# A new order of operations in the first block of a linear-attention and feed-forward kernel

## The chip, the cores and the metric

The kernel runs on one core of a Trainium2 chip. The metric is the device time of one launch in microseconds (us).

## The reference

The inputs are r, k, v of shape (4 batches, 8 heads, 768 positions, 48), a decay w and a bonus u for each head and channel, and two weight matrices, w_in (384 x 2048) and w_out (2048 x 384), all in float32. The kernel has to compute

```python
for t in range(768):                       # for each batch and head
    cur = outer(u * k[t], v[t])
    y[t] = r[t] @ (state + cur)
    state = w[:, None] * state + outer(k[t], v[t])
x = y as (3072 tokens, 384)
h = x @ w_in
g = where(h > 0, h, exp(min(h, 0)) - 1)
out = g @ w_out
```

## The kernel before

The 768 positions are cut into six token blocks of 128 positions. A block n holds 128 positions of all four batches, so 512 tokens. A *unit* (n, b) is the attention of one batch in one block. A block's feed-forward layer goes in 16 *steps* f, one for each 128 rows of the hidden layer. While the layer of one block runs, the attention of the next block is made between its matmuls. All matrices are split into a high and a low part, so every product is three matmuls.

The order of all work is written out by hand, as strings of short names that a loop reads in each step. Each engine runs its own instructions in the order in which the names stand, so a name that stands behind another on the same engine waits until that one is done. `START` makes the four units of block 0. `FIRST` is the order of each of the 16 steps of block 0's layer: it makes the units of block 1, one after the other, four steps each. Unit b has its stages 0 to 3 in the steps 4b to 4b+3, and the last character of a name is the stage in which it acts. `LATER` is the order of the steps of the blocks 1 to 5, in which the units of the blocks 2 to 5 are made at times taken from tables (`A` the step of the scores, `T` of the transposes, `Y` of the outputs, with an offset).

The names that matter, by engine:

- TensorE (PE): `hid` the hidden product of step f (9 matmuls of 512 columns), `T` the transposes of r and k of a unit, `A` its scores, `Y` its outputs, `proj` the output projection of one step before (two before from step 6 on).
- ScalarE (ACT): `neg` is a Relu and then the exponential of the hidden product, `sp` the cast that gives the high part of one weight tile (and two GpSimd instructions for the other), `gh` the high part of the activated tile, `wd` the widening of the next weights, whose data a DMA brings, `Eq` the diagonal of the odd heads' scores, `xh` the high part of x.
- VectorE (DVE): `ma` merges the halves of the weights that `wd` has widened, `r4d` the low part of a weight tile, `elu` the activation, `gl` the low part of the activated tile, `rud` the products r * u * k of a unit (two multiplies), `sum` their sum, `dr` and `dk` the decayed r and k that the scores need, `krd` the decayed k for the state, `swd` the decayed state, `pa` and `pb` the masking of a unit's scores (its outputs need both), `xl` the low part of x, `ns` the new state, `tT` transposes of a later unit.
- GpSimd (POOL): `Dp` the diagonal of the even heads' scores, `r3` the low part of the other weight tile.
- SyncE's queue (SP), which issues the DMAs one after the other: `Lw` loads the weights for five steps on (five DMAs), `rk` and `v` load r, k and v of a later unit, `mb` moves blocks of a transposed unit to DRAM (4 DMAs), `mr` gathers them again, `G` moves part of a finished x to other partitions (6 DMAs, `fill_x`), `Gl` is the same function for the last unit of a block.

The weight staging holds three pairs of tiles. `Lw` of step f needs the pair that step f has just used, and its data are widened by `wd` of step f+2. The hidden product of a block needs x of all four units of the block, with the moves of `G`. A gathered unit (`mr`) is decayed by VectorE and GpSimd one step ahead of its scores.

Of the kernel before, what the change touches and what calls it, by code (L numbers as in the profile page):

```python
# [20 lines left out]
B, H, S, D = 4, 8, 768, 48  # L21
# [29 lines left out]


FIRST = """
Eq1 rud0 hid ns3 A1 T0 ma sp sum0 neg r4d elu dk0 Y2 xh2 pb1 mbT+1 rk3 xl2 G2 mrT+1 proj gh
Dp0 pa1 dr0 r3 gl krd0 swd1 v3 rudA-2 wd Lw third tT+0
"""
LATER = """
hid AY tT+0 pbA+2 bkA-1 brA-1 proj neg elu gh gl st nsY+0 xhY+0 xlY+0 paA+1 EqA+1 krA+1 mbT+0 mrT+0 rudA-2
swA+2 sumA-1 rkY+0 vY+0 GlY+0 GY+1 DpA+0 out
"""  # L60
SCORES = [17, 20, 23, 26] + [13 + 4 * j for j in range(4, 16)]
OUTPUTS = SCORES[1:] + [77]
# [4 lines left out]
class Kernel:  # L67
# [314 lines left out]
            self.load_weights(j)  # L382

    def stages(self, n, f):
        return [(f - 4 * b, 1, b) for b in range(B) if n == 0 and 0 <= f - 4 * b < 4]

    def units_at(self, times, step):
        return [divmod(2 * B + j, B) for j, t in enumerate(times) if t == step]
# [13 lines left out]
    def step(self, n, f):  # L402
        nc = self.nc

        k = f + 2 if n == 0 else NF + 1
        units = self.stages(n, f)


        last = divmod(n * NF + f - (1 if (n, f) < EARLY else 2), NF)
        both = {  # L410
            "ru": lambda n, b: self.current(n, b),
            "kr": lambda n, b: self.key_rest(n, b),
            "A": lambda n, b: self.scores(n, b),
            "sw": lambda n, b: self.decay_state(n, b),
            "rk": lambda n, b: self.load_after(n, b, self.load_rk),
            "ns": lambda n, b: self.new_state(n, b),
            "v": lambda n, b: self.load_after(n, b, self.load_v),
            "sum": lambda n, b: self.current_sum(n, b),
            "Dp": lambda n, b: self.diag_scores(n, b, 0),
            "Dq": lambda n, b: self.diag_scores(n, b, 1),  # L420
            "Ep": lambda n, b: self.diag_scores(n, b, 0, True),
            "Eq": lambda n, b: self.diag_scores(n, b, 1, True),
            "rud": lambda n, b: self.current(n, b, nc.vector),
            "krd": lambda n, b: self.key_rest(n, b, nc.vector),
            "swd": lambda n, b: self.decay_state(n, b, nc.vector),
            "pa": lambda n, b: self.take_scores(n, b, 0),
            "pb": lambda n, b: self.take_scores(n, b, 1),
            "Y": lambda n, b: self.outputs(n, b),
            "xh": lambda n, b: self.split_x(n, b, 0),
            "xl": lambda n, b: self.split_x(n, b, 1),  # L430
            "G": lambda n, b: self.fill_x(n, b) if n == 1 or b < B - 1 else None,
            "Gl": lambda n, b: self.fill_x(n, b) if b == B - 1 else None,
        }
        by_pe = {
            "T": lambda n, b: self.turn_in(n, b),
            "dr": lambda n, b: self.decay_r(n, b),
            "dk": lambda n, b: self.decay_k(n, b),
        }
        moved = {
            "t": lambda n, b: self.turn_blocks(n, b),  # L440
            "mb": lambda n, b: self.move_blocks(n, b),
            "mr": lambda n, b: self.gather_blocks(n, b),
            "br": lambda n, b: self.decay_moved(n, b, 0),
            "bk": lambda n, b: self.decay_moved(n, b, 1),
        }
        layer = {
            "hid": lambda: self.hidden(n, f, self.rest_of(n, f)),
            "ma": lambda: self.merge(k),
            "neg": lambda: self.negative(n, f),
            "sp": lambda: self.split_w(k),  # L450
            "r4": lambda: self.rest_w(k, 1),
            "r3": lambda: self.rest_w(k, 0),
            "r4d": lambda: self.rest_w(k, 1, nc.vector),
            "r3d": lambda: self.rest_w(k, 0, nc.vector),
            "elu": lambda: self.elu(n, f),
            "gh": lambda: self.split_g(n, f, 0),
            "gl": lambda: self.split_g(n, f, 1),
            "proj": lambda: self.project(*last) if last in self.g else None,
            "Lw": lambda: [self.load_weights(j) for j in (2 * k + 2 * DEEP - 1, 2 * k + 2 * DEEP) if n == 0],
            "wd": lambda: self.widen(k + 1),  # L460
            "st": lambda: self.store(last[0]) if last[1] == NF - 1 and last[0] in self.acc else None,
            "out": lambda: self.store_next(),
            "third": lambda: self.third_slot() if (n, f) == (0, 14) else None,
            "AY": lambda: self.insertion(now),
        }
        now = n * NF + f
        for op in (LATER if n else FIRST).split():
            if op in layer:
                layer[op]()
                continue  # L470
            if op[-2] in "+-":
                name, times = op[:-3], {"A": SCORES, "Y": OUTPUTS, "T": TURNS}[op[-3]]
                for m, b in self.units_at(times, now - int(op[-2:])):
                    if (name, m, b) not in self.done:
                        self.done.add((name, m, b))
                        {**both, **moved}[name](m, b)
                continue
            name, stage = op[:-1], int(op[-1], 16)
            for at, m, b in units:
                todo = {**both, **by_pe}  # L480
                if at == stage and name in todo and (name, m, b) not in self.done:
                    self.done.add((name, m, b))
                    todo[name](m, b)
# [681 lines left out]
```

## Time and profile before

| | us |
|---|---|
| median of 3 runs | 520.05 |
| lowest and highest run | 519.72 and 521.48 |
| the profiled execution | 518.8 |
| its span, first to last instruction | 517.1 |
| TensorE busy | 499.7 |
| VectorE busy | 307.3 |
| ScalarE busy | 244.8 |
| GpSimd busy | 125.2 |

The time is that of the whole launch; the span lies inside it, from the first to the last instruction of the core. Busy times are sums over the instructions of an engine; TensorE's matmuls overlap each other, and the ends of matmuls are modelled. The mean granted clock of TensorE was 0.992 of full speed.

### The profile page before, as it was taken

Reading aid. Unit: us, or ns where it says so; the run is one execution under the profiler, and the core shown is the slowest. Engines: PE = TensorE matmul, PEld = TensorE weight load, DVE = VectorE, ACT = ScalarE, POOL = GpSimd, SP = SyncE. Lnnn points to the kernel's source line nnn. Section 1 sums busy time; section 2 is a strip of 40 time slices with the busy share of each in tenths; the row PEclk is TensorE's granted clock in tenths of the full one; section 3 lists DMA queues with packets and bytes.
Section 4 is the critical chain, followed back from the end, with each engine's and each line's share of the span. In section 5 each row is a group of like instructions: output and inputs, shape, how many; then the busy total and the mean of one; then the engine's idle time right before and its main releaser. Section 6 shows DMA issues by size and latency. Waiting matters only on the chain.

```text
span 517.1 us, 9430 instructions
## 1 busy us (share of the span) xinstructions
PE 499.7 (97%) x3584; PEld 412.7 (80%) x3584; DVE 307.3 (59%) x529; ACT 244.8 (47%) x463; POOL 125.2 (24%) x151
## 2 busy tenths in 40 slices
PE   8998997999999998999999999999999999999995
PEld 6987775878778886878888788888888887799995
DVE  5787777686667765665655765655765533433332
ACT  3267566564444454354355354454444454354442
POOL 5845546453223312112112112111011000000000
PEclk9999998999999999999999999999999999999999
DMA  9986679575854546157346156356154000011001
GB/s 134 201 169 172 121 182 179 124 137 126 153 124 99 129 103 136 45 121 150 72 83 133 46 117 137 75 97 133 46 118 113 16 10 10 1 30 25 9 0 67
DMA packets 114204, 50.92 MB, mean 98 GB/s; under 512 B 91362, under 2 KB 110052, under 8 KB 114148
## 3 DMA queue, kind: packets, MB, share of 16 engines
q1 hardware_dynamic: 102052, 45.49, 43.0%
q10 hardware_dynamic: 12096, 4.72, 3.9%
q8 instruction: 30, 0.49, 0.4%
q14 instruction: 26, 0.21, 0.1%
HBM read 35.12 MB, written 13.11 MB: 93 GB/s over the span
## 4 chain that ended last, share of the span: by engine, by line
PE 80%; DVE 7%; ACT 4%; DMA 4%; issue 2%; POOL 1%; SPq 1%; ACTq 0%; DVEq 0%; POOLq 0%
PE ps_acc L1082 35%; PE ps_h L1040 33%; PE ps_y L800 4%; PE ps_a L767 3%; DMA stage<-in_moe_w_in_dram 2%; DVE ps_h L1055 1%; PE ps_y L855 1%; PE ps_y L775 1%; DVE g L1063 1%; ACT g L1050 1%; PE ps_y L924 1%; DVE stage L563 1%; ACT g L1049 1%; ACT g L1061 1%; DMA rk<-blocks 1%
## 5 line engine op out<-in xcount | busy, mean ns | idle before, releaser
L1040 PE MATMUL ps_h<-x,wh 128*128 128x512 f32 (+1 forms) x588 | 180.9, 389 | 2.1 <-DMA x<-x 1.8
L1082 PE MATMUL ps_acc<-g,wh 128*128 128x512 f32 x480 | 167.3, 403 | 0.0
L1055 DVE SCALAR_TENSOR_TENSOR ps_h<-g,ps_h 128x512 f32<-128x512 f32 x96 | 66.6, 693 | 120.9 <-ACT g L1050 120.9
L1040 PEld LDWEIGHTS ps_h<-x,wh 128*128 128x128 f32 x588 | 109.1, 188 | 27.0 <-DVE g L1063 3.2
L1040 PE MATMUL ps_h<-x,wl 128*128 128x512 f32 (+1 forms) x294 | 113.6, 386 | 0.6 <-DVE wl L601 0.6
L1049 ACT ACTIVATE g<-ps_h 128x512 f32<-128x512 f32 x96 | 57.2, 596 | 115.4 <-PE ps_h L1040 103.3
L1082 PEld LDWEIGHTS ps_acc<-g,wh 128*128 128x128 f32 x480 | 90.8, 189 | 21.8 <-issue 1.1
L1063 DVE TENSOR_TENSOR g<-ps_h,g 128x512 fp32r<-128x512 f32 x96 | 66.3, 690 | 54.8 <-ACT g L1061 54.1
L1061 ACT CAST g<-ps_h 128x512 fp32r<-128x512 f32 x96 | 56.3, 586 | 82.9 <-DVE ps_h L1055 82.9
L1082 PE MATMUL ps_acc<-g,wl 128*128 128x512 f32 x240 | 94.6, 394 | 0.0
L1040 PEld LDWEIGHTS ps_h<-x,wl 128*128 128x128 f32 x294 | 55.2, 188 | 12.7 <-DVE wl L601 0.8
L1050 ACT ACTIVATE g<-g 128x512 f32<-128x512 f32 x96 | 60.7, 632 | 3.1
L819 POOL TENSOR_TENSOR a<-ident,diag 128x512 f32<-128x512 f32 x20 | 20.9, 1044 | 150.2 <-PE ps_y L800 131.8
L1082 PEld LDWEIGHTS ps_acc<-g,wl 128*128 128x128 f32 x240 | 45.6, 190 | 9.1
L660 POOL TENSOR_TENSOR tb<-rk,qw 128x512 f32<-128x512 f32 x16 | 21.8, 1361 | 78.8 <-DMA rk<-blocks 55.3
L1082 PE MATMUL ps_acc<-wh,g 128*128 128x384 f32 x128 | 35.0, 337 | 0.1
L574 POOL TENSOR_SCALAR stage<-stage 128x384 f32<-128x384 f32 x16 | 19.7, 1231 | 42.4 <-DVE stage L563 42.4
L826 DVE COPY_PREDICATED a<-mask,ps_a 128x512 f32<-128x512 int32 x40 | 27.4, 728 | 0.0
L815 ACT ACTIVATE a<-ident,diag 128x128 f32<-128x128 f32 x80 | 25.5, 393 | 0.0
L767 PEld LDWEIGHTS ps_a<-stage,tb 48*64 48x64 f32 x512 | 20.3, 133 | 5.6 <-issue 5.3
L767 PE MATMUL ps_a<-stage,tb 48*64 48x128 f32 x512 | 24.7, 273 | 0.0
L1082 PEld LDWEIGHTS ps_acc<-wh,g 128*128 128x128 f32 x128 | 23.4, 188 | 1.2 <-issue 0.5
(128 smaller groups left out, 488.0 us busy)
## 6 DMA issues: line engine op xcount, KB each, us to landing
blocks<-tb SPq DMA_DIRECT2D x64, 128.0 KB, 2.3
rk<-blocks SPq DMA_DIRECT2D x16, 512.0 KB, 3.6
stage<-in_moe_w_out_dram SPq DMA_DIRECT2D x16, 383.8 KB, 4.9
stage<-in_moe_w_in_dram SPq DMA_DIRECT2D x32, 143.7 KB, 4.6
out_dram<-stage ACTq DMA_DIRECT2D x80, 48.0 KB, 1.7
r_t<-in_r_dram SPq DMA_DIRECT2D x17, 192.0 KB, 4.5
k_t<-in_k_dram SPq DMA_DIRECT2D x17, 192.0 KB, 5.2
v_t<-in_v_dram SPq DMA_DIRECT2D x17, 192.0 KB, 5.3
```

The source lines that it names most:

```text
L660: (self.nc.gpsimd if i else self.nc.vector).tensor_mul(dst, src, by)
L767: nc.tensor.matmul(un["pa"][i][keys, a * P : (a + 1) * P], lhsT=un["k"][rows, a, keys], rhs=un["r"][rows, a, :], start=True, stop=True, sk ...
L815: self.nc.scalar.activation(un["a"][i][:, a, :], self.ident, AF.Copy, scale=diag[:, a : a + 1])
L819: self.nc.gpsimd.tensor_mul(un["a"][i], self.ident.unsqueeze(1).to_broadcast([P, HP, P]), diag.unsqueeze(2).to_broadcast([P, HP, P]),)
L826: self.nc.vector.copy_predicated(un["a"][i], self.mask.bitcast(I32).unsqueeze(1).to_broadcast([P, HP, P]), un["pa"][i].rearrange("p (a t) ...
L1040: self.nc.tensor.matmul(ph[:, part], lhsT=a[:, c * P : (c + 1) * P], rhs=x[:, c, part], start=(c == 0 and i == 0), stop=(c == NC - 1 and i ...
L1049: nc.scalar.activation(g, ph, AF.Relu, scale=-1.0)
L1050: nc.scalar.activation(g, g, AF.Exp, scale=-1.0)
L1055: self.nc.vector.scalar_tensor_tensor(ph, g, -1.0, ph, op0=ALU.add, op1=ALU.max)
L1061: nc.scalar.copy(part, g)
L1063: nc.vector.tensor_sub(part, g, self.g[n, f][2].bitcast(F32))
L1082: self.nc.tensor.matmul(at, lhsT=lhs, rhs=rhs, start=(f == 0 and i == 0), stop=(f == NF - 1 and i == 2),)
```

## The change

In `FIRST`, four things change their place.

- `sp` (the weights' cast) and `r4d` stood ahead of `elu`, and `sp` ahead of `neg`; now the order is `neg`, `elu`, `sp`, `r4d`. On ScalarE the Relu and the exponential come ahead of the cast, on VectorE the activation ahead of the weights' low part.
- VectorE's work for a unit is spread: `rud` of the units 1 to 3 goes to the end of the step ahead of stage 0 (`rudx`), `krd` from stage 0 to stage 1, `swd` from stage 1 to stage 2. The first unit keeps `rud` in stage 0.
- `gh` stands ahead of `xh` on ScalarE. On VectorE `gl` stands ahead of `xl`, of both masks `pa` and `pb`, and of both decays `dk` and `dr`; before, it stood behind them. The first unit has both decays (`df`) ahead of `elu`.
- `proj` stands after `mr` in the text; on TensorE its place among the matmuls is the same.

In `LATER`, `Gl` is moved from behind the loads `rk` and `v` to a place ahead of `mr`, and it now serves all units from (2, 3) on. Before, only the last unit of a block was served by `Gl`, and the others by `G` one step later.

```diff
 FIRST = """
-Eq1 rud0 hid ns3 A1 T0 ma sp sum0 neg r4d elu dk0 Y2 xh2 pb1 mbT+1 rk3 xl2 G2 mrT+1 proj gh
-Dp0 pa1 dr0 r3 gl krd0 swd1 v3 rudA-2 wd Lw third tT+0
+Eq1 hid ns3 A1 T0 rud0 ma sum0 neg df0 elu sp r4d Y2 gh gl xh2 xl2 pa1 pb1 dk0 dr0 mbT+1 rk3 G2 mrT+1
+proj krd1 swd2 Dp0 r3 rudx v3 rudA-2 wd Lw third tT+0
 """
 LATER = """
-hid AY tT+0 pbA+2 bkA-1 brA-1 proj neg elu gh gl st nsY+0 xhY+0 xlY+0 paA+1 EqA+1 krA+1 mbT+0 mrT+0 rudA-2
-swA+2 sumA-1 rkY+0 vY+0 GlY+0 GY+1 DpA+0 out
+hid AY tT+0 pbA+2 bkA-1 brA-1 proj neg elu gh gl st nsY+0 xhY+0 xlY+0 paA+1 EqA+1 krA+1 mbT+0 GlY+0 mrT+0 rudA-2
+swA+2 sumA-1 rkY+0 vY+0 GY+1 DpA+0 out
 """
...
-        return [(f - 4 * b, 1, b) for b in range(B) if n == 0 and 0 <= f - 4 * b < 4]
+        return [(f - 4 * b, 1, b) for b in range(B) if n == 0 and -1 <= f - 4 * b < 4]
...
-            "G": lambda n, b: self.fill_x(n, b) if n == 1 or b < B - 1 else None,
-            "Gl": lambda n, b: self.fill_x(n, b) if b == B - 1 else None,
+            "G": lambda n, b: self.fill_x(n, b) if (n, b) < (2, B - 1) else None,
+            "Gl": lambda n, b: self.fill_x(n, b) if (n, b) >= (2, B - 1) else None,
...
-            "dr": lambda n, b: self.decay_r(n, b),
-            "dk": lambda n, b: self.decay_k(n, b),
+            "dk": lambda n, b: self.decay_k(n, b) if b else None,
+            "dr": lambda n, b: self.decay_r(n, b) if b else None,
+            "df": lambda n, b: self.decay_in(n, b) if b == 0 else None,
...
-            name, stage = op[:-1], int(op[-1], 16)
+            name, stage = op[:-1], -1 if op[-1] == "x" else int(op[-1])
```

## Rows read from the trace of the kernel before

**Rows 1.** TensorE's waits, whole span: waiting line, releaser, us in total, times, longest.

```profile
PE ps_a L741 <- DVE rk L672: 5.9, 3, 3.3
PE ps_h L1040 <- DMA x<-x: 1.8, 2, 1.6
```

**Rows 2.** Windows, the stretch of step 9: length, busy by engine, PEclk, DMA share, GB/s.

```profile
80.67:92.36 11.69, 8.35 (x35) 6.57 (x35) 9.70 (x17) 7.47 (x15) 6.54 (x7) 0.72 1.15 228
```

**Rows 3.** TensorE's timeline: start, us, line, operation, count, idle before and releaser.

```profile
86.34 2.08 PE L741 MATMUL ps_a<-rk 48*128 48x128 f32 x16 [3.33 <-DVE rk L672]
88.35 0.79 PE L1082 MATMUL ps_acc<-g,wh 128*128 128x512 f32 x1
...
123.93 0.68 PE L1040 MATMUL ps_h<-x,wh 128*128 128x512 f32 x2
...
206.33 0.70 PE L1040 MATMUL ps_h<-x,wh 128*128 128x512 f32 x2 [1.58 <-DMA x<-x]
```

**Rows 4.** VectorE's timeline, steps 6, 8, 13 and 29.

```profile
67.57 1.35 DVE L826 COPY_PREDICATED a<-mask,ps_a 128x512 f32<-128x512 int32 x2
...
80.53 0.55 DVE L703 TENSOR_TENSOR ru<-r_t,u_b 128x384 f32<-128x384 f32 x1
...
81.59 0.95 DVE L563 SCALAR_TENSOR_TENSOR stage<-stage,wide 128x768 int32<-128x768 int32 x1
...
84.31 0.69 DVE L1055 SCALAR_TENSOR_TENSOR ps_h<-g,ps_h 128x512 f32<-128x512 f32 x1 [0.59 <-ACT g L1050]
...
85.52 0.68 DVE L672 TENSOR_TENSOR rk<-ps_rT,pw 128x512 f32<-128x512 f32 x1
...
116.41 0.69 DVE L624 STREAM_TRANSPOSE tb<-r_t 128x512 f32<-128x512 f32 x1
...
196.80 0.75 DVE L951 TENSOR_TENSOR x<-ps_y,x 128x256 fp32r<-128x256 f32 x2 [0.50 <-ACT x L949]
```

**Rows 5.** ScalarE's timeline: `wd` and `Eq` of step 4, `wd` 5, `neg` and `gh` 8, `wd` 9.

```profile
63.07 1.08 ACT L554 ACTIVATE wide<-stage 128x768 f16<-128x768 bf16 x1 [0.60 <-DMA stage<-in_moe_w_in_dram]
64.02 1.25 ACT L815 ACTIVATE a<-ident,diag 128x128 f32<-128x128 f32 x4
...
69.29 1.08 ACT L554 ACTIVATE wide<-stage 128x768 f16<-128x768 bf16 x1 [1.01 <-DMA stage<-in_moe_w_in_dram]
...
83.03 0.59 ACT L1049 ACTIVATE g<-ps_h 128x512 f32<-128x512 f32 x1
...
85.04 0.58 ACT L1061 CAST g<-ps_h 128x512 fp32r<-128x512 f32 x1 [0.76 <-DVE ps_h L1055]
...
91.68 1.08 ACT L554 ACTIVATE wide<-stage 128x768 f16<-128x768 bf16 x1 [0.47 <-DMA stage<-in_moe_w_in_dram]
```

**Rows 6.** SyncE's queue, DMA issues: start, us for all of the count.

```profile
51.43 4.33 SPq L959 DMA_DIRECT2D x<-x  x6
...
74.53 4.51 SPq L959 DMA_DIRECT2D x<-x  x6
...
81.13 0.43 SPq L219 DMA_DIRECT2D stage<-in_moe_w_in_dram  x1
...
97.94 4.32 SPq L959 DMA_DIRECT2D x<-x  x6
...
120.10 3.79 SPq L959 DMA_DIRECT2D x<-x  x6
...
198.24 0.34 SPq L641 DMA_DIRECT2D rk<-blocks  x1
...
201.81 4.05 SPq L959 DMA_DIRECT2D x<-x  x6
```

**Rows 7.** DMA packets from 36 to 135 us; then issues from 79.1 and from 120, us to landing.

```profile
DMA packets 25766, 15.32 MB, mean 155 GB/s; under 512 B 17165, under 2 KB 23935, under 8 KB 25758
...
stage<-in_moe_w_in_dram SPq DMA_DIRECT2D x2, 47.9 KB, 3.8
...
x<-x SPq DMA_DIRECT2D x6, 16.0 KB, 1.8
```

## The prediction, made before the change was run

> **What bounds the kernel now.** I read the page first: TensorE is busy for 499.7 of 517.1 us, at a mean clock of 0.992. So only its waits and slow stretches can be won. Its list of waits is short [rows 1]: 5.9 us in three waits of a unit's scores for VectorE's decayed r, and 1.8 us in two waits of a block's first hidden product for x's moves. The timeline puts them in place [rows 3]. The longest, 3.33 us, ends at 86.34 in step 9. After it TensorE runs at a low clock: 0.72 as the mean of the stretch [rows 2], and the 16 score matmuls take 2.08 us. From 86.34 to that stretch's end at 92.36 are 6.0 us; at the 1.2 GHz level this work takes nearly twice what it takes at 2.4, so up to 3.0 us are lost there. I take 2.7. The other two score waits (steps 1 and 5) are 5.9 - 3.3 = 2.6 us together. Block 0 thus offers 5.9 + 2.7 = 8.6 us, the later blocks 1.8.
>
> VectorE and ScalarE show why the score wait arises. In step 8 the first instruction of `rud` starts at 80.53, the merge at 81.59, `elu` at 84.31, `dr` at 85.52, which ends at 86.20 and releases the scores [rows 4]. The Relu starts at 83.03 [rows 5], since the cast stands ahead of it and waits for the merge, and the merge stands behind `rud` and behind the last step's `gl`.
>
> The third view is SyncE's queue. x's moves start at 51.43, 74.53, 97.94 and 120.10 [rows 6], a period of 22.2 to 23.4 us for four steps. The loads of the same step stand behind the six moves, and `wd` waits for them two steps later: it starts at 63.07 and 69.29, and again at 91.68, each time released by a DMA [rows 5].
>
> **Part one, what the new order of block 0 takes away.** The Relu no longer waits for merge and cast. In stage 0 VectorE loses two multiplies of `rud` and one of `krd`, 3 x 0.55 = 1.65 us [rows 4], to steps 3 and 1 of a unit, which hold less. `dr` no longer stands behind a late `elu`. Each of the three score waits would go, or shrink to about 1 us in step 9. The cast itself, moved behind the exponential, is hidden by `elu` on VectorE; if that cover were gone it would cost under 0.6 us, `gh`'s 0.58 being the nearest row [rows 5]. `swd` in stage 2 stands behind `xl` and ahead of the next step's `ns`; nothing on TensorE waits for it soon. `proj` keeps its place on TensorE: nothing.
>
> **Part two, what is late next.** Two edits put work ahead of the outputs: both masks now stand behind `gl`, so behind `gh` too. Follow the chain from `wd` in stage 0, which stands on ScalarE ahead of the diagonal and of the next Relu. From its start: `wd` to the diagonal 0.95 (64.02 - 63.07), the diagonal 1.25, Relu to `elu` 84.31 - 83.03 = 1.28, `elu` to `gh` 85.04 - 84.31 = 0.73, `gh` 0.6, `gl` 0.6 (as `rud`'s kind), both masks 1.35 [rows 4, 5]. Sum 6.75 us until the outputs of the unit can be made. The same way from `wd` of stage 1, released by the next loads, to the next start of x's moves: 0.95 + 1.28 + 0.73 + 0.6 + 0.6 + `xl` 0.75 = 4.9 us.
>
> Now the loads. `wd` of step 4 starts 63.07 - 51.43 = 11.6 us after x's moves started, that of step 5 69.29 - 51.43 = 17.9, that of step 9 91.68 - 74.53 = 17.15 [rows 5, 6]. For step 8 the last load was issued at 81.13 and landed 3.8 later [rows 6, 7]: 84.9, which is 10.4. These distances are the DMAs' own (six moves of 0.7 us, then loads on full engines), so the change doesn't shorten them; between 10.4 and 11.6 I take 10.7 for the later cycles.
>
> The first moves: step 1 saves its score wait (1.4 of the 2.6), but the outputs of step 2 need masks that now stand behind `gl`, and ScalarE has `wd` and the diagonal ahead of that Relu. I give the first moves 51.2, 0.2 earlier (bounds 0 and 1.4). Then:
>
> - `wd` 4 at 51.2 + 11.6 = 62.8, masks done 69.6; `wd` 5 at 51.2 + 17.9 = 69.1, moves at 74.0 (before 74.53).
> - `wd` 8 at 74.0 + 10.7 = 84.7, masks done 91.4; `wd` 9 at 74.0 + 17.15 = 91.15, moves at 96.05 (before 97.94).
> - `wd` 12 at 96.05 + 10.7 = 106.75, masks done 113.5. Behind them VectorE has `krd` 0.5, two transposes 1.25, the last merge 0.45 (half size), then `elu` to `gh` 0.73, `gh` 0.6, `gl` 0.6, `xl` 0.75: moves at 118.4 (before 120.10).
>
> Block 1's first product starts with the landing of the fourth of these moves: 120.10 + 3 x 0.63 + 1.8 = 123.8 against 123.93 [rows 3, 6, 7]. So block 0 ends 1.7 us earlier, not 8.6. Before the outputs of steps 2, 6, 10 and 14 TensorE, which no longer waits for the scores, should wait: by what is won at the scores and not kept, some 1 to 2 us each, in two pieces, one for each mask.
>
> **Part three, x's moves ahead of the gathering.** At 206.33 block 2's first product waits 1.58 us for x's moves, issued at 201.81, behind the gathering at 198.24 and three loads [rows 3, 6]. `xl` is done at 196.80 + 0.75 = 197.55 [rows 4], so the moves can start there, 4.2 us earlier, more than the wait: 1.6 won, and the other such wait, 0.2 [rows 1], goes the same way. Behind the moves stand the gathering and the loads of r, k and v, later by 197.55 + 4.05 - 198.24 = 3.4 us. Their users come about a four-step period later, so I cost this at nothing; were the slack under 3.4 us, eleven units would pay the rest.
>
> A page of the Trainium skill would make the loads a smaller matter. The rows show full DMA engines (share 1.15) at 228 GB/s [rows 2], and 17165 of 25766 packets under 512 bytes [rows 7]. "DMA: Bandwidth & Descriptors", section Bandwidth, gives 341 GB/s for a 1 MB transfer; by it the loads take two thirds, `wd` waits for no DMA, and, as ScalarE could start `wd` 5 and 9 about 1.4 us sooner, the sum would be 2.8 us lower, 513.6. The same page wants 512 bytes for the full rate (section Specifications), so the row holds here.
>
> **The sum.** 1.7 + 1.6 + 0.2 = 3.5 us. The profiled execution took 518.8 us, 1.7 beyond its span, and would take 515.3. It lies 1.25 below the median of the three runs, so against that: 520.05 - 3.5 = 516.5.
>
> **The rivals.** *The loads do not pace it.* If they land sooner in the new order or the first moves come 1.4 earlier, each cycle moves up. All 8.6 of block 0 plus 1.8 gives 520.05 - 10.4 = 509.7; half of block 0, 514. For it: VectorE and ScalarE are not full. Against: three starts of `wd` at a DMA's landing.
>
> *Block 0 gives nothing.* If each cycle's loads land 0.6 later than taken, the three cycles lose 1.8, and only part three is left: 518.2. For it: x's moves start sooner but the loads behind them meet r, k and v on full engines.
>
> *Slower, by the clock ahead of the last outputs.* For step 14 I take a wait of 1.3 us out of those 1 to 2. If the load for `wd` 12 lands 2 us later still, the wait is 3.3, as long as the one after which the clock fell [rows 3]. Then the two projections and the hidden product up to block 1 lose the 2.7 as well: 1.7 - 2 - 2.7 = -3 in block 0, +1.8 later, 521.3; at 3 us, 522.3. Below 2 us it only eats the gain; from there it decides. Against: no load in rows 5 was later than the 11.6 or 17.9 us that the sum uses.
>
> *The later moves pay nothing*, since a load or the queue holds them: 516.5 + 1.8 = 518.3.
>
> **How the numbers follow.** Forecast 0.50, with its own range 515 to 518; loads not pacing 0.18, 509.7 to 515; block 0 gives nothing 0.16, 517.5 to 519.5; slower by the clock 0.10, 520.5 to 523; later moves idle 0.06. About 0.3% (1.6 us) is what a measurement here can tell, so faster means below 518.5: 0.50 + 0.18 + half of 0.16 + 0.01, about 0.77. Same 0.14, slower 0.09. From 511.5 to 519.4 some 0.8 is held; 0.1 lies on either side.
>
> **What would show it.** Right: no score wait over 1.5 us, clock 1.0 around step 9, new waits of the outputs on the masks (`copy_predicated`) at steps 2, 6, 10, 14; `wd` still released by DMAs 10 to 12 us after x's moves; these at about 51, 74, 96 and 118; no wait at block 2's start. Wrong: moves 20.8 us apart or less and no output waits (the first rival), or a clock drop after an output wait.

## The result, and the profile after

The changed kernel took 516.48 us (median of 5 runs, 515.29 to 517.08), the kernel before 520.5 us beside it (5 runs). The ratio is 0.9917, with a 95% interval of 0.9896 to 0.9937: 4.0 us, and by the interval 3.3 to 5.4. The forecast was 516.5. The profiled execution took 515.29 us with a span of 513.5, against 518.8 and 517.1 before. Here and below, ratios and intervals leave out the few launches over 1.5% slower than a kernel's fastest, and they are not exactly the quotients of the medians.

The waits of TensorE in the changed kernel (waiting line, releaser, us in total, times, longest), which answer to [rows 1]:

```profile
PE ps_a L742 <- DVE rk L673: 3.1, 2, 2.4
PE ps_y L909 <- DVE a L827: 2.3, 4, 0.9
...
PE ps_h L1041 <- ACT g L1062: 0.7, 1, 0.7
```

The waits for x's moves at the starts of blocks 2 and 3 are gone. Those for the scores shrank from 5.9 to 3.1 us, and four waits of the outputs for the masks are new, 2.3 us together. The windows view of the stretch of [rows 2]:

```profile
80.67:92.36 11.69, 8.43 (x73) 6.34 (x73) 7.53 (x13) 6.02 (x12) 6.52 (x7) 1.00 1.19 216
```

The granted clock is 1.00 where it was 0.72; the DMA engines are as full as before. TensorE's timeline, which answers to [rows 3], shows where the new waits lie:

```profile
68.18 0.65 PE L909 MATMUL ps_y<-rk,state 48*64 48x128 f32 x12 [0.44 <-DVE a L827]
...
84.06 1.16 PE L742 MATMUL ps_a<-rk 48*128 48x128 f32 x16 [2.41 <-DVE rk L673]
...
90.82 0.65 PE L909 MATMUL ps_y<-rk,state 48*64 48x128 f32 x12 [0.85 <-DVE a L827]
...
122.48 0.70 PE L1041 MATMUL ps_h<-x,wh 128*128 128x512 f32 x2 [0.73 <-ACT g L1062]
...
203.63 0.63 PE L1041 MATMUL ps_h<-x,wh 128*128 128x512 f32 x2
```

Step 9 still waits 2.41 us for its scores, but the 16 score matmuls take 1.16 us instead of 2.08. That and the clock of 1.00 are no fixed gain of the change: in a second execution of the same kernel, below, the clock falls behind this wait as it did before. Block 1 starts at 122.48 (before 123.93), block 2 at 203.63 without a wait (before 206.33, after 1.58 us of one).

VectorE's timeline around that score wait, which answers to [rows 4], and GpSimd's in the same stretch:

```profile
77.58 0.55 DVE L704 TENSOR_TENSOR ru<-r_t,u_b 128x384 f32<-128x384 f32 x1
78.16 1.28 DVE L705 TENSOR_TENSOR ru<-ru,k_t 128x384 f32<-128x384 f32 x1
79.36 0.95 DVE L564 SCALAR_TENSOR_TENSOR stage<-stage,wide 128x768 int32<-128x768 int32 x1
...
80.69 0.68 DVE L1056 SCALAR_TENSOR_TENSOR ps_h<-g,ps_h 128x512 f32<-128x512 f32 x1
81.29 0.55 DVE L602 SCALAR_TENSOR_TENSOR wl<-stage,wh 128x384 fp32r<-128x384 f32 x1
...
83.23 0.68 DVE L673 TENSOR_TENSOR rk<-ps_rT,pw 128x512 f32<-128x512 f32 x1
```

```profile
77.62 1.41 POOL L600 TENSOR_TENSOR wl<-stage,wh 128x384 fp32r<-128x384 f32 x1
80.40 1.24 POOL L575 TENSOR_SCALAR stage<-stage 128x384 f32<-128x384 f32 x1 [1.38 <-DVE stage L564]
```

The two multiplies of `rud` (L704, L705) now carry the name `rudx` and belong to the step ahead. In VectorE's order they stand where they stood: behind the last `gl` and right ahead of the merge (L564). The second one takes 1.28 us beside GpSimd's subtraction (L600); it took 0.56 in the kernel before.

ScalarE's timeline, `wd` in stages 0 and 1 of two units, and SyncE's queue; they answer to [rows 5] and [rows 6]:

```profile
62.08 1.07 ACT L555 ACTIVATE wide<-stage 128x768 f16<-128x768 bf16 x1 [2.29 <-DMA stage<-in_moe_w_in_dram]
...
68.49 1.08 ACT L555 ACTIVATE wide<-stage 128x768 f16<-128x768 bf16 x1 [1.72 <-DMA stage<-in_moe_w_in_dram]
...
84.72 1.07 ACT L555 ACTIVATE wide<-stage 128x768 f16<-128x768 bf16 x1 [2.73 <-DMA stage<-in_moe_w_in_dram]
...
91.49 1.08 ACT L555 ACTIVATE wide<-stage 128x768 f16<-128x768 bf16 x1 [2.08 <-DMA stage<-in_moe_w_in_dram]
```

```profile
50.74 4.39 SPq L960 DMA_DIRECT2D x<-x  x6
...
73.44 4.80 SPq L960 DMA_DIRECT2D x<-x  x6
...
96.44 4.60 SPq L960 DMA_DIRECT2D x<-x  x6
...
118.57 3.78 SPq L960 DMA_DIRECT2D x<-x  x6
...
196.61 3.78 SPq L960 DMA_DIRECT2D x<-x  x6
200.56 0.46 SPq L642 DMA_DIRECT2D rk<-blocks  x1
```

`wd` waits 1.7 to 2.7 us for its load at each of these starts. In the kernel before it waited 0.60 and 1.01 us in the first unit [rows 5], and in the second nothing in stage 0 (at 85.52) and 0.47 in stage 1. ScalarE became free sooner and met the same loads. x's moves are 22.70, 23.00 and 22.13 us apart; before they were 23.10, 23.41 and 22.16. In the later blocks the moves go out at 196.61, ahead of the gathering at 200.56. The DMA packets from 36 to 135 us, and the landing of x's moves there, hardly changed from [rows 7]:

```profile
DMA packets 25606, 15.10 MB, mean 153 GB/s; under 512 B 17158, under 2 KB 23806, under 8 KB 25598
...
x<-x SPq DMA_DIRECT2D x24, 16.0 KB, 1.8
```

### The profile page after: what moved, and what is told of

It reads as the page before. It is cut to its first block, busy times and chain, and to the rows that moved or that the text cites. A ratio compares the mean times of both kernels' runs of the same rounds, so it can differ in the third digit from the quotient of the medians.

```text
span 513.5 us, 9437 instructions
## 1 busy us (share of the span) xinstructions
PE 495.8 (97%) x3584; PEld 409.7 (80%) x3584; DVE 315.0 (61%) x529; ACT 244.4 (48%) x463; POOL 126.7 (25%) x151
## 4 chain that ended last, share of the span: by engine, by line
PE 74%; DVE 6%; DMA 5%; SPq 5%; ACT 3%; issue 2%; POOL 2%; ACTq 0%; DVEq 0%; POOLq 0%
PE ps_acc L1083 33%; PE ps_h L1041 31%; DMA stage<-in_moe_w_in_dram 4%; PE ps_y L801 4%; PE ps_a L768 3%; SPq L960 1%; PE ps_y L776 1%; DVE ps_h L1056 1%; SPq L218 1%; SPq L173 1%; PE ps_y L925 1%; ACT g L1062 1%; DVE g L1064 1%; ACT g L1051 1%; POOL stage L575 1%
## 5 line engine op out<-in xcount | busy, mean ns | idle before, releaser
L661 POOL TENSOR_TENSOR tb<-rk,qw 128x512 f32<-128x512 f32 x16 | 21.3, 1330 | 128.7 <-DMA rk<-blocks 111.9
```

The source lines that it names most:

```text
L661: (self.nc.gpsimd if i else self.nc.vector).tensor_mul(dst, src, by)
```

## The experiments

In the diffs, "-" is the changed kernel. Each kernel was timed beside the kernel before, and its ratio is against that.

**One part alone.** The first kernel has the new block 0 and the old later blocks; the second has the old block 0 and x's moves ahead of the gathering. The diff is that of the first; in the second, all the edits but these are undone.

```diff
-hid AY tT+0 pbA+2 bkA-1 brA-1 proj neg elu gh gl st nsY+0 xhY+0 xlY+0 paA+1 EqA+1 krA+1 mbT+0 GlY+0 mrT+0 rudA-2
-swA+2 sumA-1 rkY+0 vY+0 GY+1 DpA+0 out
+hid AY tT+0 pbA+2 bkA-1 brA-1 proj neg elu gh gl st nsY+0 xhY+0 xlY+0 paA+1 EqA+1 krA+1 mbT+0 mrT+0 rudA-2
+swA+2 sumA-1 rkY+0 vY+0 GlY+0 GY+1 DpA+0 out
...
-            "G": lambda n, b: self.fill_x(n, b) if (n, b) < (2, B - 1) else None,
-            "Gl": lambda n, b: self.fill_x(n, b) if (n, b) >= (2, B - 1) else None,
+            "G": lambda n, b: self.fill_x(n, b) if n == 1 or b < B - 1 else None,
+            "Gl": lambda n, b: self.fill_x(n, b) if b == B - 1 else None,
```

> Only the new order of block 0; x's moves of the later blocks stand behind the loads again, as before. Pacing theory (block 0 is paced by the circle of x's moves, loads, widening, masks and x's moves again): block 0 ends 1.5 us earlier and the waits at the starts of blocks 2 and 3 (1.6 and 0.2 us) stay, so 518.9, and 1.5 to 2 us over the whole change. Rival (the whole gain is the later moves', block 0 gives nothing): 520.5. Rival (the whole gain is the new order's, since the wait at block 2 would have been hidden anyway): 516.5.

> Only x's moves ahead of the gathering in the later blocks; block 0 in its old order. Pacing theory: the two waits at the starts of blocks 2 and 3 go and nothing else changes, 1.8 us under before, 518.7. Rival (block 0 gives nothing): 516.5. Rival (the later moves pay nothing): 520.5.

Block 0 alone: 518.83 us against 519.68, ratio 0.9962 (0.9936 to 0.9988). The later blocks alone: 515.73, ratio 0.9922 (0.9894 to 0.9949). So 0.85 and 3.95 us by the medians, where 1.7 and 1.8 had been forecast; by the ratios 2.0 (0.6 to 3.3) and 4.1 (2.7 to 5.5). The first came out as expected (518.9). The second missed its 518.7 by 3 us and lies nearest to the rival by which block 0 gives nothing (516.5). By its time the whole change can't be told from the later blocks alone (0.9917 against 0.9922). That block 0 gives something rests on the run of the first kernel and on the traces below. TensorE's timeline of the first kernel, at the starts of the blocks 2 and 3:

```profile
206.16 0.70 PE L1041 MATMUL ps_h<-x,wh 128*128 128x512 f32 x2 [2.00 <-DMA x<-x]
...
285.39 0.70 PE L1041 MATMUL ps_h<-x,wh 128*128 128x512 f32 x2 [0.54 <-DMA x<-x]
```

Its block 1 starts at 122.81, 1.1 us ahead of the profiled kernel before, but block 2 starts only 0.2 ahead: the wait for x's moves has grown to 2.00 us. In this trace, without the second part, most of what block 0 wins is waited away one block later. In the second kernel block 1 starts late, at 124.34, and block 2 at 205.07 without a wait.

**The kernels again.** The changed kernel once more, and the kernel before three times, for what one profiled execution tells.

> The changed kernel as it is, beside the next two on the same chip, and a second trace of it. Pacing theory: 516.5, block 1's first product within 0.5 us of the first trace's 122.5, no wait for x's moves at any block's start. Rival (the later moves alone carry the whole gain, as their run of 515.7 suggests): the time is that of the later moves alone, 515.7, though block 0 ends 1.5 us sooner than in the old order.

> The kernel before as it is, for a second trace. If the waits for x's moves at the starts of blocks 2 and 3 vary from run to run, they are above the first trace's 1.6 and 0.2 us when the time is near the median of its runs (519.7 to 520.5), and the later moves' gain in the medians (3.9 us) is explained by them. Rival: the waits are the same 1.8 us in all, and the gain of the later moves alone stays larger than the traces show.

> The kernel before, for a third trace. If its waits for x's moves vary from run to run, a run near the median of 519.7 to 520.5 shows more than 1.8 us of them. Rival: the same 1.8, and the difference between runs lies elsewhere, ahead of block 0's layer or in the end.

> The kernel before, for a fourth trace, with the same two expectations as the third: over 1.8 us of waits for x's moves in a run near the median, or the same 1.8 and a difference elsewhere.

The changed kernel: 515.33 us against 519.99, ratio 0.9898 (0.9874 to 0.9923). The later blocks alone had 0.9922 (0.9894 to 0.9949), and the intervals overlap, so the rival of this run isn't excluded by times. In the second trace of the changed kernel the score wait of step 9 is

```profile
84.44 2.08 PE L742 MATMUL ps_a<-rk 48*128 48x128 f32 x16 [3.13 <-DVE rk L673]
```

and the clock behind it is 0.50, the 1.2 GHz level, from 84 to 90 us. All the same block 1 starts no later than in the first trace.

The kernel before, one execution each: 518.21, 520.94 and 517.74. Their waits for x's moves are 1.7, 2.1 and 1.5 us: the longer the run, the longer the waits. But none of the three fell in the 519.7 to 520.5 that was asked about, so that question stays open. With the traces of the two parts there are five of the old block 0 and three of the new one. Block 1 starts at

```
old order  123.93 123.17 123.72 122.86 124.34   mean 123.60
new order  122.48 122.39 122.81                 mean 122.56
```

which is 1.0 us, with a spread of 1.5 within the old order. Part of both lies ahead of block 0's steps, in code that the change leaves alone: the first hidden matmul of the steps starts at 35.87 to 36.66 us in the old order (mean 36.23) and at 35.70 to 36.26 in the new (mean 35.95). From there to block 1's start the old order takes 87.00 to 87.68 us (mean 87.38) and the new 86.55 to 86.69 (mean 86.61). So block 0 itself gives 0.8 us, and no trace of one order reaches into the other. From the start of block 1 to that of block 5 the old later blocks take 316.14, 316.34, 318.34, 316.12 and 317.41 us (mean 316.87), the new ones 314.32, 314.81 and 313.90 (mean 314.34): 2.5 us. The 318.34 has a reason of its own. The windows view of that trace, the third of the kernel before:

```profile
200.00:210.00 10.00, 8.15 (x32) 6.24 (x32) 5.62 (x9) 3.81 (x9) 1.29 (x1) 0.90 0.59 112
210.00:220.00 10.00, 10.00 (x109) 8.19 (x108) 5.97 (x10) 3.40 (x6) 2.03 (x2) 0.93 0.21 54
```

Its wait for x was 1.85 us at 206.68, and the granted clock behind it 0.90 and 0.93 where the first trace has 1.00 in both stretches; block 2 took 80.55 us where the other four took 78.7 to 79.2. So the wait that part three removes can cost more than its own length.

**The loads ahead of x's moves.** In block 0 the six moves of the first three units go behind the weight loads of the same step.

```diff
-proj krd1 swd2 Dp0 r3 rudx v3 rudA-2 wd Lw third tT+0
+proj krd1 swd2 Dp0 r3 rudx v3 rudA-2 wd Lw Gw2 third tT+0
...
-            "G": lambda n, b: self.fill_x(n, b) if (n, b) < (2, B - 1) else None,
+            "G": lambda n, b: self.fill_x(n, b) if (1, B - 2) < (n, b) < (2, B - 1) else None,
+            "Gw": lambda n, b: self.fill_x(n, b) if b < B - 1 else None,
```

> The whole change, and in block 0 x's moves of the first three units stand behind the weight loads of their step in the DMA queue, not ahead of them. Pacing theory: the widening in stage 0 no longer waits for its load (2.3 to 2.7 us in each of three cycles), the masks come earlier, the outputs' waits go, and the scores' wait of step 9 shrinks; 513.5 (512 to 515). Rival (VectorE's and ScalarE's own work in their order sets the end of block 0): the widening's waits go but the time stays at 516.5.

512.29 us, ratio 0.9852 (0.9813 to 0.9890), as the theory had it (513.5, 512 to 515). ScalarE's timeline of this kernel, `wd` of stage 1 and of the next stage 0, and SyncE's queue:

```profile
67.85 1.08 ACT L556 ACTIVATE wide<-stage 128x768 f16<-128x768 bf16 x1 [3.12 <-DMA stage<-in_moe_w_in_dram]
...
81.23 1.07 ACT L556 ACTIVATE wide<-stage 128x768 f16<-128x768 bf16 x1
```

```profile
54.04 4.81 SPq L961 DMA_DIRECT2D x<-x  x6
...
75.36 4.86 SPq L961 DMA_DIRECT2D x<-x  x6
...
96.98 3.78 SPq L961 DMA_DIRECT2D x<-x  x6
...
114.52 3.78 SPq L961 DMA_DIRECT2D x<-x  x6
```

Stage 0's `wd` no longer waits for a load; stage 1's still does, by 3.1 us. Moves are 21.3 and 21.6 us apart, the last ones start at 114.52 instead of 118.57, and block 1 at 118.72 instead of 122.48. The loads behind x's moves were what held block 0 of the changed kernel.

**x's moves twice.** Each of the six moves of three units of block 1 is issued a second time, to the same place.

```diff
-                self.nc.sync.dma_start(x[FILLS[i], :, c], x[rows, :, NC])
+                for _ in range(2 if n == 1 and b < B - 1 else 1):
+                    self.nc.sync.dma_start(x[FILLS[i], :, c], x[rows, :, NC])
```

> The whole change, and in block 0 each of the six moves of x of the first three units is issued twice (18 small DMAs more in all). Pacing theory: the loads behind the moves come 4.4 us later in each of three cycles with no slack to take it up; the next moves start at 77.8 and 105, not 73.4 and 96.4, block 1 starts near 135, and the time is 529 (525 to 531). Rival (loads do not pace block 0): at most 2 us more, 518.

548.42 us, ratio 1.0559 (1.0511 to 1.0606), far more than the 529 expected. SyncE's queue, ScalarE and TensorE in this kernel:

```profile
50.91 15.75 SPq L961 DMA_DIRECT2D x<-x  x12
...
84.93 15.19 SPq L961 DMA_DIRECT2D x<-x  x12
```

```profile
73.39 1.06 ACT L555 ACTIVATE wide<-stage 128x768 f16<-128x768 bf16 x1 [13.43 <-DMA stage<-in_moe_w_in_dram]
```

```profile
79.47 1.12 PE L909 MATMUL ps_y<-rk,state 48*64 48x128 f32 x12 [11.58 <-DVE a L827]
```

Twelve moves take 15.0 to 15.75 us of the queue, not twice the 4.4 to 4.8 of six: 11.4, 10.4 and 10.4 us more in the three cycles, 32.2 together. SyncE's list of waits (its queue's line, releaser, us in total, times, longest) says why:

```profile
SPq L961 <- DMA x<-x: 22.8, 19, 2.0
```

Of these, 18 waits and 21.8 us lie in block 0, where the changed kernel has none: the second move of a pair is issued only when the first has landed. The kernel is 32 us slower than the changed one (548.42 - 516.48). What is added to x's moves comes out at the end nearly one to one, through `wd`, the masks and the outputs: the expectation had the price of the second move wrong, and the chain right.

**Less of the new waits.** One kernel puts the masks ahead of `gh` and `gl`, as they stood relative to `gl` before; another makes `rud` two steps ahead.

```diff
-Eq1 hid ns3 A1 T0 rud0 ma sum0 neg df0 elu sp r4d Y2 gh gl xh2 xl2 pa1 pb1 dk0 dr0 mbT+1 rk3 G2 mrT+1
+Eq1 hid ns3 A1 T0 rud0 ma sum0 neg df0 elu sp r4d Y2 pa1 pb1 gh gl xh2 xl2 dk0 dr0 mbT+1 rk3 G2 mrT+1
```

> The whole change, but both masks stand ahead of the low part of the activation on VectorE in block 0. Pacing theory: the outputs of steps 2, 6, 10 and 14 lose their waits on the masks (2.3 us by the list of waits), but x's moves start when they did, so block 1 starts within 0.5 us of the change's 122.5 and the time stays at 516.5 (515.8 to 517). Rival (the masks' place costs what the outputs wait): 514.0.

```diff
-        return [(f - 4 * b, 1, b) for b in range(B) if n == 0 and -1 <= f - 4 * b < 4]
+        return [(f - 4 * b, 1, b) for b in range(B) if n == 0 and -2 <= f - 4 * b < 4]
...
-            name, stage = op[:-1], -1 if op[-1] == "x" else int(op[-1])
+            name, stage = op[:-1], -2 if op[-1] == "x" else int(op[-1])
```

> The whole change, but the two multiplies r * u * k of the units 1 to 3 at the end of the second step ahead of stage 0 (stage 2 of the unit before), not of the step ahead, where they stand in VectorE's order just where they stood before the change. Pacing theory: the scores' wait of step 9 falls from 2.4 to 1.0 to 1.4 us, x's moves start when they did, and the time is that of the whole change within 0.7 us. Rival (the scores' waits set the end of block 0): 1.2 us less than the whole change.

The masks: 515.04 us, ratio 0.9914 (0.9882 to 0.9945). `rud` two ahead: 515.77, ratio 0.9921 (0.9893 to 0.9950). Neither can be told from the changed kernel (0.9917 and 0.9898), though the masks' 515.04 lies under the 515.8 to 517 expected. TensorE's timeline, first of the kernel with the masks ahead, then of the one with `rud` two ahead:

```profile
84.00 2.08 PE L742 MATMUL ps_a<-rk 48*128 48x128 f32 x16 [3.22 <-DVE rk L673]
```

```profile
70.33 1.12 PE L909 MATMUL ps_y<-rk,state 48*64 48x128 f32 x12 [2.22 <-DVE a L827]
```

With the masks ahead all output waits are gone, and step 9's score wait is 3.22 us at a low clock (0.76 from 80 to 94 us); with `rud` two ahead that score wait is gone, and an output wait of 2.22 us stands in its place, with 0.76 from 66 to 80. Block 1 starts at 122.07 and 122.56 all the same. TensorE waits for the same loads in whichever place its order meets them.

**Both.** The loads ahead and `rud` two ahead, which joins two diffs above; and the loads ahead with x's moves one step later, in stage 3, behind that step's loads too, and r, k and v of the later unit behind these. The diff is that of the second; its `G` and `Gw` are as above.

```diff
-Eq1 hid ns3 A1 T0 rud0 ma sum0 neg df0 elu sp r4d Y2 gh gl xh2 xl2 pa1 pb1 dk0 dr0 mbT+1 rk3 G2 mrT+1
-proj krd1 swd2 Dp0 r3 rudx v3 rudA-2 wd Lw third tT+0
+Eq1 hid ns3 A1 T0 rud0 ma sum0 neg df0 elu sp r4d Y2 gh gl xh2 xl2 pa1 pb1 dk0 dr0 mbT+1 G2 mrT+1
+proj krd1 swd2 Dp0 r3 rudx rudA-2 wd Lw Gw3 rk3 v3 third tT+0
```

> The loads ahead of x's moves in block 0, and the two multiplies two steps ahead. Pacing theory: with the loads out of the way the scores' wait of step 9 (2.3 us) lies on the path; it falls to about 1.2 us, block 1 starts 1 us sooner than with the loads ahead alone (118.7), and the time is 511.3. Rival (the next limit is another): 512.3, as with the loads ahead alone.

> The loads ahead of x's moves, and a step further: in block 0, x's moves, and the loads of r, k and v, stand behind the weight loads of stage 3 too. Pacing theory: with the loads ahead of the moves in stage 2 alone, the widening of stage 1 still waits 3.1 and 3.0 us for loads that stand behind the moves; now they go, x of block 1 is ready sooner, and block 1 starts 1 to 2 us sooner than 118.7, time 511.0. Rival (what is left is set by VectorE's and TensorE's work): the waits go, the time stays at 512.0.

511.65 us, ratio 0.9855 (0.9817 to 0.9892), and 512.01, ratio 0.9852 (0.9817 to 0.9887): no better than the loads ahead alone. With `rud` two ahead the score wait of step 9 stayed at 2.35 us, not the 1.2 expected: once its multiplies were out of the way the merge itself took 1.45 us, behind a wait of 0.36 for a weight load. In the second kernel `wd` of stage 1 no longer waits, but one of stage 2 does, 1.87 us at 73.72. The execution profiled of it was its longest, 515.03; step 9 in TensorE's timeline:

```profile
84.37 2.08 PE L743 MATMUL ps_a<-rk 48*128 48x128 f32 x16 [2.31 <-DVE rk L674]
```

Its clock is low behind that wait (0.76 from 80 to 94 us), and block 1 starts at 122.42, as in the changed kernel. Some of this lies ahead of block 0's steps: they begin at 37.15 us, behind another stretch of low clock (0.50 from 33 to 36), and at 36.22 and 35.79 in the two other kernels with the loads ahead. Block 0 itself takes 82.50 us with the loads ahead alone (clock 1.00 throughout), 83.26 with `rud` two ahead as well (0.88 from 78 to 92) and 85.26 here. So with the loads out of the way a low clock seems to cost time that it doesn't cost in the changed kernel (86.58 us at 1.00, 86.69 with the low stretch). These are single traces of different kernels: that the clock makes the difference is argued, not shown.

## Why the prediction was right, and where its terms were off

**The mechanism.** That weight loads behind x's moves pace block 0 held for the changed kernel: the run with the loads ahead and the one with the moves twice show it. The moves came at 50.74, 73.44, 96.44 and 118.57 where 51.2, 74.0, 96.05 and 118.4 stood in the working. The chain from stage 1's `wd` to the next moves was 4.95 us twice (68.49 to 73.44, 91.49 to 96.44), forecast 4.9; from `wd` 12 to the last moves 11.4, forecast 11.65. Moving the loads changed the time by 3.0 to 4.2 us (512.29 against 515.33 and 516.48); moving the masks or `rud`, which TensorE waits for directly, changed nothing that can be measured.

For the kernel before, the same pacing is not shown. No run moves the loads in the old order, and in the later part of its block 0 the profile speaks against it: the `wd` at 97.76, 103.58, 109.32 and 114.91 wait for no load, and TensorE has no wait of its own from 86.34, the end of the score wait, to block 1.

The step from x's fourth move to block 1's start was a near coincidence. In the changed kernel the sum holds: 118.57 + 3 x 0.63 + 1.8 = 122.26, and block 1 came at 122.48 after a wait of 0.73 (the releaser that the list names, `gh`, ends at 122.32, and the product doesn't read it). But TensorE's timelines of the kernel before and of the one with the loads ahead show no wait there:

```profile
123.70 0.40 PE L1082 MATMUL ps_acc<-g,wh 128*128 128x512 f32 x1
...
118.72 0.63 PE L1042 MATMUL ps_h<-x,wh 128*128 128x512 f32 x2
```

In the first the last projection matmul, at 123.70, runs straight into block 1 at 123.93 [rows 3]; in the second the same sum gives 118.21 and block 1 starts 0.5 us later. There TensorE's own matmuls behind the last outputs set the start.

**Block 0's gain, forecast 1.7, was 1.45 between the two profiled executions, 1.0 over all traces of either order, and 0.8 without what lies ahead of its steps.** By the ratio of its own run it was 2.0 (0.6 to 3.3), which excludes none of these. The mis-sized terms are the loads' distances in the second cycle, taken as 10.7 and 17.15 us and measured as 84.72 - 73.44 = 11.28 and 91.49 - 73.44 = 18.05. The working followed the second cycle of the one execution (10.4 and 17.15); the first cycle's 11.6 and 17.9 were nearer. By this "block 0 gives nothing" was partly true: its condition was loads 0.6 later than taken. The first moves made up for some of it, 0.46 us earlier on the means (51.26 to 50.80), not 0.2. The three cycles together became only 0.6 shorter (means 68.47 and 67.86), because the circle through stage 1's `wd` was there before: 69.29 - 51.43 = 17.86 and 5.24 to the moves, now 17.75 and 4.95. Also, the profiled kernel before was one of its later ones (123.93 against the mean of 123.60).

**The score wait of step 9, forecast at about 1 us, was 2.41.** In the second execution it was 3.13. So the sign "no score wait over 1.5 us" failed in both, and "clock 1.0 around step 9" in the second. The step that failed is that stage 0 loses 1.65 us of VectorE's work. Only `krd`'s 0.55 left it. `rud` at the end of the step ahead is the same place in VectorE's order, and it grew by 0.7 us beside GpSimd. This cost nothing at the end, since the loads decide. The output waits came at the steps named, but were 2.3 us in all, where 1 to 2 us each had been forecast. The score wait kept part of the rest. They also came in one piece, not two: from stage 0's `wd` both masks were done after 6.66 us (107.17 to 113.83, and alike in the two units before), as the forecast 6.75 had it, but TensorE waited for the first mask only, since the 0.65 us of matmuls behind it covered the second.

**The 2.7 us of low clock in "block 0 offers 8.6" weren't there to be won** while loads pace it: with the drop block 1 starts at 122.07 to 122.56 (masks ahead, the kernel again, `rud` two ahead), without it at 122.48. Block 0's own length is 86.58 us without the drop and 86.69 with it in the changed kernel. In the kernel before block 1 starts at 122.86 with the score matmuls at 2.08 us, and at 123.17 with them at 1.16 and a shorter low stretch behind.

**The later moves, forecast 1.8, gave 2.5 in the traces.** The waits removed were 1.5 to 2.5 us in five traces of the old order (1.8 is the one read), and in one of the five the clock behind the wait cost another 1.3 to 1.8 (80.55 against 78.7 to 79.2). From block 1's start to the end of the span the gain is 2.9 us (means 393.9 and 391.0). By the medians this part alone gave 3.95 us, with an interval of 2.7 to 5.5; the rest of that, if there is one, stays open. The gathering and the loads behind the moves were late for nobody: block 3 and block 4 take 78.5 and 76.3 us before and after, so the cost of nothing held.

So the total was right with 1.0 + 2.5 in place of 1.7 + 1.8 in the traces: two errors against each other. That 516.5 was met to 0.02 us is luck besides: it was 3.5 us below a median of 520.05, the measured 516.48 is 4.0 below one of 520.5, and the same kernel later took 515.33. The variant with faster loads, 513.6 in the prediction (520.05 - 3.5 - 2.8 is 513.75), did not come: `wd` waited longer for its loads than before, at 216 GB/s on engines as full. The slower rival needed an output wait of 3.3 us ahead of block 1; the last of the output waits was 0.31 (at 113.27).

## What to carry to other kernels

When TensorE's waits name VectorE, follow the chain back to what releases each engine in turn: if it closes in a circle through a queue, a new order of the work in between only moves the wait along the circle, and the transfer that stands ahead in the queue is what to move. Moving an instruction to "the end of the step before" is no move if nothing stands between on its engine. A term read from one execution (a wait, a distance between DMA and use) deserves the spread of several before a gain of 1 us is built on it.

## What the runs showed of the hardware that was not expected

VectorE's multiply of two inputs took 1.28 us instead of 0.56 while GpSimd's subtraction ran, and that took 1.41 where it takes 1.02 to 1.05 in the kernel before; it was the same for the next unit (1.27 at 101.17). The Trainium skill, "SBUF — State Buffer", section "SBUF: two separate sides", says that VectorE with two inputs in SBUF and a GpSimd instruction that reads SBUF share a pair of ports, held by whichever starts first for the whole instruction. The trace agrees for these two, but not everywhere: `r4d` at 81.29, with two inputs as well, took its plain 0.55 us while GpSimd's scaling (80.40 to 81.64) still ran. It is no matter of a rough span: in the kernel before `r4d` ran at 43.42 for 0.56 us wholly inside such a scaling (42.89 to 44.12). The lines are GpSimd's and VectorE's:

```profile
42.89 1.23 POOL L574 TENSOR_SCALAR stage<-stage 128x384 f32<-128x384 f32 x1 [2.35 <-DVE stage L563]
```

```profile
43.42 0.56 DVE L601 SCALAR_TENSOR_TENSOR wl<-stage,wh 128x384 fp32r<-128x384 f32 x1 [0.62 <-ACT wh L577]
```

Where the Trainium skill and the measurement differ, the measurement decides. The scaling reads one input from SBUF, the subtraction two; that this makes the difference was not tried.

A wait of TensorE doesn't tell by its length whether the clock falls. After 2.22, 2.31, 3.13 and 3.22 us it was low (0.76 in the 14 us around), after 1.88 (new block 0 alone) and 2.35 it was low for a shorter while (0.88), after 2.32 and 2.41 it stayed at 1.00. After 3.32 in the second trace of the kernel before the score matmuls still took 1.16 us and the clock fell only behind them (0.88), and they took 2.08 after 3.34 in the two others. At block 2's start 1.85 us was followed by 0.90, 2.00 us (the kernel with the new block 0 alone) by 1.00.

In this kernel a second DMA to the same place is not a second transfer of the same price: it is issued after the first has landed (21.8 us of such waits in 18 issues of block 0), and 12 moves took 15.0 to 15.75 us of SyncE's queue where six take 4.4 to 4.8.
